# Late products of layer two's gated mixer: stores on POOL's queue, earlier requests for mixing blocks and bias rows, and the last row turned between two products

## The chip, the cores and the metric

The kernel runs on one core of a Trainium2 chip. The engines of a core work side by side: TensorE multiplies matrices (PE in the profile, and PEld for its weight loads), VectorE (DVE), ScalarE (ACT) and GpSimd (POOL) work on tiles, and SyncE (SP) only issues transfers between the chip's memory and the core's on-chip memory. Each engine takes its instructions in the order in which the program wrote them for it, and waits on semaphores for the others. The metric is device time of one execution in microseconds, lower is better; what is given is the median of several runs.

## The reference

Four blocks run one after the other on an input x of 2048 rows by 512 features: a linear attention block, a gated mixer, and the same two again with the same weights. Only the second mixer ("layer two", L = 1 in the kernel) is touched by the change. The mixer, in the reference's own words:

```python
def _B_ref(x, w_in, w_sp, b_sp, w_out):
    Fh = F // 2                                             # 896
    z = _gelu(jnp.einsum("bsd,df->bsf", x, w_in))
    z1 = z[..., :Fh]
    z2 = _layernorm(z[..., Fh:], axis=-1)
    g = jnp.einsum("ts,bsf->btf", w_sp, z2) + b_sp[None, :, None]
    return jnp.einsum("bsf,fd->bsd", z1 * g, w_out)
...
x = x + _A_ref(_layernorm(x, axis=-1), A_wqkv, A_wo)
x = x + _B_ref(_layernorm(x, axis=-1), B_w_in, B_w_sp, B_b_sp, B_w_out)
```

Everything is float32. So z1 (the gate) and z2 (what is mixed) are two halves of one product of x with `w_in`; z2 is normalised row by row; then the 2048 by 2048 matrix `w_sp` mixes all rows of z2, a bias per row is added, the result is multiplied by z1 and goes through `w_out`.

## The kernel before

**Numbers in two parts.** TensorE takes each float32 operand as a high part h (rounded, written by ACT in `high`, L213) and a low part l = x - h (written by DVE in `low`, L216). A product is three matmuls: h with h, h with l, l with h (L227 to L229 in `mm3`, L1142 to L1144 in `fmul`, L983 to L985 in `emul`, L1833 to L1835 in `acc`). Many products are also formed by Strassen's scheme with seven products of half size in place of eight (numbered r = 1 to 7 in the code), which need sums and differences of blocks first.

**Memory.** On-chip memory is given out by hand in slots that are used in turn, oldest free one first: 22 pages of 128 by 512 (`pages`, pg), 6 quads of four pages (`quads`, qd), 4 big ones (`bigs`, bg), the 16 tiles `ztile`, one for each 128 rows (z_z, z_y and z_q in the profile), and the 8 accumulator banks (`banks`). A new user of a slot waits for every reader and writer of the old one, transfers included.

**Order.** The program is one list written out by hand; there is no planner. Each engine and each queue executes its part of the list in that order, so an instruction that waits holds up everything behind it on its own engine. Plain transfers are issued by SP (`nc.sync.dma_start`). POOL issues those that convert the type or add (`nc.gpsimd.dma_start`), among them the loads of `w_in` parts in `load_r` (L202 to L205), which `wfetch` calls for two pages at a time.

**The stage around the change.** `P2.run2` goes through row blocks s = 1 to 18 of layer two. Odd steps are `odd`, even ones from 8 on are `epair`, which forms z2 of two row blocks and takes a list of callbacks to run between its products. Rows are turned (transposed) for the products: most through a store and a load in another shape, some, among them the last row block 15, on TensorE (`transposes`, L383), with a copy by DVE (L433), the high part by ACT and the low part by DVE (`d_high`, `d_low`). At the last odd step, s = 17, `odd` starts the products u[1] and u[2] of the third row group in `first_a` (each a product of six matmuls and a copy by ACT, L1159), adds the two halves of the third row group in `raw(0)` (DVE, L1149), turns row block 15 (through `q`, at its old place after `first_a(1, 2)`), and then finishes u[1] and u[2] in `first_b`. The last `epair`, s = 18, calls `late4`, which applies the gelu to them and stores them (`first_out`, `out`), and `late3`.

Then `P4.run` drives `P2.tail`, the late products: the last third of z1 for the last two row groups. `tail` is a generator with three stops. Its products are the six matmuls of `fmul` per f in 0, 1, 2 with five left operands one after the other (T5, T6, T7, x and T4), after a first product in `f`. After the first stop it applies gelu to c[0..2] and stores them, after the second to y[0..2], after the third to d[0..2], nine stores, all through `out` (L1130 to L1136) and before the change all issued by SP in L1134. The y and d results go into four spare pages, `room` (`Rooms`, handed out in turn): three y and the first d fill it, and the second and third d reuse places. Between the second and the third stop the last two tiles of z2, 14 and 15, are normalised by `e4` (L371, ACT).

At each stop `P4.run` prepares the mixing: `zahead` (`zsum` on DVE, L1728 to L1734, then `zpart`, ACT and DVE) prepares an operand from z2; `sp` (`wsp`, L1663 ACT and L1664 DVE) splits a mixing block into high and low part, in a quad of its own; `fetch` (L1643) asks SP for the next mixing blocks, 512 KB each. A raw block occupies half a quad (`Halves`), and its half is free again when `sp` has split it. The mixing products themselves are `mm`, step g = 0, 1, 2, ..., of twelve matmuls each (L1833 to L1835). In the loop over g, step g asks for block g + 5 and splits block g + 2 where that isn't done. The four bias rows are loaded by `loadb` (L1864, 256 KB each) at g = 0, and first needed when DVE adds them to the sums at the end of g = 3 (L1797).

Of the kernel before, what the change touches and what calls it, by code (L numbers as in the profile page):

```python
# [13 lines left out]
OP = mybir.AluOpType  # L14
# [5 lines left out]
NT = S // P  # L20
# [131 lines left out]
def mixer_kernel(ctx: ExitStack, tc: tile.TileContext, x_in, wqkv, wo_d, win1_d, win2_d, wsp_d, bsp_d, wout_d,  # L152
                 ident_d, mask_d, out_d):
    nc = tc.nc
# [7 lines left out]
    pages = Slots(main, "pg", 22)  # L162
    quads = Slots(main, "qd", 6)
    bigs = Slots(main, "bg", 4)
    banks = Banks(psum, "bank", 8)

    PAGE = [P, 512]
    ztile = {}
# [22 lines left out]
    z1s = {}  # L191
# [20 lines left out]
    def high(h, src):  # L212
        nc.scalar.activation(h, src, AF.Copy)  # L213
# [610 lines left out]
    class P2:  # L824
# [302 lines left out]
            nc.sync.dma_start(z1s[self.L, n, f], t)  # L1127
            home.put(t)

        def out(self, n, f, b, home=pages):  # L1130
            t = home.get(PAGE) if hasattr(home, "get") else home
            self.mark = nc.scalar.activation(t, b, AF.Gelu_apprx_tanh)
            z1s[self.L, n, f] = dram.tile(PAGE, F32, name=f"z1_{self.L}_{n}_{f}")
            nc.sync.dma_start(z1s[self.L, n, f], t)  # L1134
            if t is not home:
                home.put(t)  # L1136

# [29 lines left out]

        def first_out(self, *fs):
            for f in fs:
                self.out(2, f, self.u[f])  # L1170
                banks.done(self.u[f])
                if f:
                    self.wfetch()

        def T1(self):
            h, l = (t.bitcast(F32)[:, 0:2] for t in self.xT[3])
            t = self.B[:, 0]
            nc.vector.tensor_sub(t, h, t)
            nc.vector.tensor_add(t, t, l)
# [17 lines left out]
        def tail(self):  # L1197
            V, A = nc.vector, nc.scalar.activation
            h, l = (t.bitcast(F32) for t in self.xT[3])
            big = [bigs.get([P, NF, 512], F32R if k < 2 else F32) for k in range(3)]  # L1200
            c = [big[2][:, f] for f in range(3)]
            room = Rooms(big[2][:, f] for f in range(3, NF))
            two = lambda k, n: big[k][:, 2 * n:2 * n + 2]
            self.T |= {6: (two(0, 0), two(0, 1)), 7: (two(0, 2), two(1, 0)), 4: (two(1, 1), two(1, 2))}
            b21 = self.B[:, 1]
            for r, t in ((6, self.t2), (7, self.b22)):
                for k in range(2):
                    high(self.T[r][0][:, k], t[k])
                for k in range(2):
                    low(self.T[r][1][:, k], t[k], self.T[r][0][:, k])  # L1210
            for k in range(2):
                V.tensor_sub(b21[:, k], b21[:, k], self.t2[k])
            pages.put(*self.t2, *self.b22)
            self.f(True)
            ws, d = [], []
            for f in range(3):
                ws.append(self.ws.popleft())
                v = banks.get(PAGE)
                self.fmul(v, [t[:, 0:256] for t in ws[f]], self.T[5], True, True)
                A(c[f], v, AF.Copy)  # L1220
                banks.done(v)
            quads.put(self.T1q)
            self.fout()
            for f in range(3):
                y = self.y[f]
                self.fmul(y, [t[:, 256:512] for t in ws[f]], self.T[6], False, False)
                pages.put(*ws[f])
                self.wfetch()
                d.append(banks.whole(PAGE))
                A(d[f], y, AF.Copy)  # L1230
                V.tensor_add(y, y, c[f])
            split(*self.T[4], b21)
            self.e3(NT - 2)
            self.e3(NT - 1)
            self.e4(NT - 4)
            self.e4(NT - 3)
            quads.put(self.B)
            ws = []
            for f in range(3):
                ws.append(self.ws.popleft())  # L1240
                self.fmul(d[f], [t[:, 0:256] for t in ws[f]], self.T[7], False, False)
                V.tensor_add(c[f], d[f], c[f])
            yield
            for f in range(3):
                self.out(3, f + 3, c[f], c[f])
            x = [t[:, 2:4] for t in self.xT[3]]
            for f in range(3):
                self.fmul(self.y[f], [t[:, 256:512] for t in ws[f]], x, False, True)
                pages.put(*ws[f])
            yield  # L1250
            for f in range(3):
                self.out(3, f, self.y[f], room)
                banks.done(self.y[f])
            quads.put(*self.xT.pop(3))
            self.e4(NT - 2)
            self.e4(NT - 1)
            for f in range(3):
                w = self.ws.popleft()
                self.fmul(d[f], w, self.T[4], False, True)
                pages.put(*w)  # L1260
            yield
            for f in range(3):
                self.out(2, f + 3, d[f], room)
                banks.done(d[f])
            bigs.put(*big)

# [73 lines left out]
        def odd(self, s, p, q, r):  # L1340

            p()
            if s == NT - 1:
                self.first_a(0)
            if s == NT + 1:
                self.first_a(1, 2)
                self.B = quads.get([P, 2, 2, 512])
                self.raw(0)
            elif s - 5 >= FIRSTPAIR:
                self.e3(s - 5)  # L1350
                self.e3(s - 4)
            n = FILL.get(s, 0)
            if n:
                self.f(s == NT - 1, ZHome(s + 1) if s + 1 < NT else pages)
            if s == NT - 1:
                self.d_high(s - 2)
                self.d_low(s - 2)
            else:
                r()
            q()  # L1360
            if s - 4 < FIRSTPAIR:
                self.e4(s - 4)
            self.dsum(s - 3)
            self.dsplit(s - 3)
            if n > 2:
                self.f(home=ZHome(s + 2) if s + 2 < NT else pages)
            if n > 1:
                self.f(True)
            if s == NT - 1:
                self.first_b(0)  # L1370
                self.first_out(0)
            if s == NT + 1:
                self.first_b(1, 2)
                self.T1()
# [222 lines left out]
    class P4:  # L1597
# [559 lines left out]
        def run(self, nxt):  # L2157
            p2 = self.p2
            early = nxt is None
# [7 lines left out]
            n = 0  # L2167
            if early:
                for _ in p2.tail():
                    n += 1  # L2170
                    self.zahead(n - 1)
                    self.sp(n - 1)
                    if n < 3:
                        self.fetch(n + 1)
                self.zahead(3)
                self.fetch(5)
            while p2.f():
                self.zahead(min(self.zmade, 3))
                n += 1
# [11 lines left out]
            n = len(self.steps)  # L2191
            for g in range(n):
                p, k = self.steps[g]
                self.fetch(g + 5)
                evac_first = p == "P6" and k == HT - 1
                div_first = p in self.div and k == 13 and p == "P4"
                if not evac_first and not div_first:
                    self.sp(g + 2)
                    self.zahead(g + 4 if p in ("P2", "P1") else g + 4)
                self.mm(g)  # L2200
                if evac_first:
                    self.evac(p)
                    self.sp(g + 2)
                if not early and g == 14:
                    self.sums.fetch()
                if not early and 15 <= g <= 15 + LEFT:
                    self.sums.tick()
                if nxt is not None:
                    self.sums.halve(PARTS.get((p, k), -1), self.mark)
                if g == 0:  # L2210
                    self.loadb()
                if p in self.div:
                    if k % 2 == 1:
                        self.evac_div(p, self.SEVEN[k // 2])
                    if div_first:
                        self.sp(g + 2)
                    if k == 13 and p == "P4":
                        self.gq.extend((n, f) for n in range(2) for f in range(3))
                    continue
                if p == "P1" and k == 6:  # L2220
                    self.ask(3)
                self.tick()
                if p == "P3":
                    if k == FIRST:
                        self.first()
                self.wseven(p, k)
                if p == "P7" and k == HT - 1 and self.div:
                    self.sp(g + 3)
                if k == HT - 1 and not evac_first:
                    self.evac(p, (0,) if p == "P3" else (0, 1))  # L2230
# [82 lines left out]
```

## Time and profile before

| what | value |
|---|---|
| median of 3 runs | 1356.5 us (1356.29 to 1357.22) |
| the profiled execution's own time | 1356.72 us |
| its span in the profile | 1354.8 us |
| granted TensorE clock, mean | 0.999 |
| PE busy | 1345.7 us, 99% of the span |
| DVE busy | 1040.5 us, 77% |
| ACT busy | 717.2 us, 53% |
| POOL busy | 442.9 us, 33% |

The profile's times count from the start of the span. In a timeline a row gives start, duration, engine, line of the kernel, operation, the tiles written and read by name, and how many instructions of a kind are put together; in brackets stands how long the engine had sat idle before, and what ended that. Matmuls overlap, so a matmul is listed with 0.39 us although the next one starts much sooner: the distance between starts is what counts. SPq rows are the issue of a transfer, not the transfer.

### The profile page before, as it was taken

How to read it: one execution, taken by the hardware profiler on the slowest of the kernel's cores; microseconds unless marked ns; L12 is line 12 of the kernel's file. 1: busy time of each engine (PE TensorE's matmuls, PEld its weight loads, DVE VectorE, ACT ScalarE, POOL GpSimd, SP SyncE). 2: the span in 40 equal slices, each digit the busy share in tenths (PEclk: the TensorE clock that was granted, in tenths of full speed). 3: DMA queues.
4: the chain of work that ended last, by engine and by line, in shares of the span. 5: the costliest groups of instructions: out<-in, count | busy, mean ns of one | idle time of the engine just before them, and what ended most of it. 6: DMA issues, size and time to landing. Idle time of an engine off the chain costs nothing.

```text
span 1354.8 us, 19111 instructions
## 1 busy us (share of the span) xinstructions
PE 1345.7 (99%) x6564; PEld 1147.4 (85%) x6564; DVE 1040.5 (77%) x1640; ACT 717.2 (53%) x1199; POOL 442.9 (33%) x581
## 2 busy tenths in 40 slices
PE   9999999999999999999999999999999999999998
PEld 7888888888888888889988888888887888888898
DVE  6679877763796788898867878677678757988885
ACT  5774534433642364445667756565686333734454
POOL 3765775444031400201335334545430021021021
PEclk9999999999999999999999999999999999999999
DMA  5898587877877966533766513778647543455344
GB/s 182 280 320 274 162 273 249 294 271 255 288 248 256 279 201 182 192 132 63 173 179 202 181 53 119 234 226 272 209 149 267 166 170 126 155 186 173 107 73 68
DMA packets 161777, 267.21 MB, mean 197 GB/s; under 512 B 13712, under 2 KB 53136, under 8 KB 161552
## 3 DMA queue, kind: packets, MB, share of 16 engines
q1 hardware_dynamic: 148144, 240.04, 53.2%
q0 software_dynamic: 13536, 25.96, 9.3%
q8 instruction: 51, 0.84, 0.2%
q14 instruction: 46, 0.38, 0.1%
HBM read 187.30 MB, written 87.03 MB: 202 GB/s over the span
## 4 chain that ended last, share of the span: by engine, by line
PE 95%; DVE 1%; ACT 1%; DMA 1%; issue 1%; SPq 0%; DVEq 0%; ACTq 0%
PE bank L229 14%; PE bank L227 14%; PE bank L228 14%; PE bank L1834 13%; PE bank L1835 13%; PE bank L1833 13%; PE bank L2031 3%; PE bank L2032 3%; PE bank L2033 3%; PE bank L983 1%; PE bank L985 1%; PE bank L984 1%; PE bank L383 1%; PE bank L2045 1%; PE bank L2044 1%
## 5 line engine op out<-in xcount | busy, mean ns | idle before, releaser
L1834 PE MATMUL bank<-qd,pg 128*128 128x512 f32 x768 | 299.7, 390 | 1.2 <-DVE qd L1664 1.2
L1833 PE MATMUL bank<-qd,pg 128*128 128x512 f32 x768 | 299.4, 390 | 1.4 <-ACT qd L1663 1.4
L1835 PE MATMUL bank<-qd,pg 128*128 128x512 f32 x768 | 299.3, 390 | 0.0
L1663 ACT ACTIVATE qd<-qd 128x1024 fp32r<-128x1024 f32 x136 | 143.1, 1053 | 132.6 <-PE bank L1835 117.9
L1664 DVE TENSOR_TENSOR qd<-qd,qd 128x1024 fp32r<-128x1024 f32 x136 | 171.5, 1264 | 54.1 <-ACT qd L1663 53.7
L229 PE MATMUL bank<-qd,pg 128*128 128x512 f32 x448 | 174.7, 390 | 0.0
L1833 PEld LDWEIGHTS bank<-qd,pg 128*128 128x128 f32 x768 | 144.6, 188 | 32.0 <-ACT qd L1663 1.8
L1834 PEld LDWEIGHTS bank<-qd,pg 128*128 128x128 f32 x768 | 144.6, 188 | 31.3 <-DVE qd L1664 1.5
L1835 PEld LDWEIGHTS bank<-qd,pg 128*128 128x128 f32 x768 | 144.6, 188 | 29.8
L1874 POOL TENSOR_TENSOR bg<-bg,pg 128x512 f32<-128x512 f32 x28 | 50.3, 1798 | 304.2 <-ACT qd L1663 174.1
L227 PE MATMUL bank<-qd,pg 128*128 128x512 f32 x308 | 120.2, 390 | 0.2 <-ACT pg L213 0.2
L228 PE MATMUL bank<-qd,pg 128*128 128x512 f32 x308 | 120.0, 390 | 0.0
L229 PEld LDWEIGHTS bank<-qd,pg 128*128 128x128 f32 x448 | 84.1, 188 | 18.2 <-DVE pg L216 0.4
L362 POOL TENSOR_SCALAR rs<-mv 128x1 f32<-128x1 f32 x80 | 24.6, 308 | 192.3 <-DVE mv L360 179.3
L371 ACT ACTIVATE pg<-pg,nb,rs 128x512 f32<-128x512 f32 x52 | 42.1, 811 | 85.1 <-POOL nb L365 79.4
L1573 POOL TENSOR_TENSOR pg<-pg,pg 128x512 f32<-128x512 f32 x48 | 67.1, 1398 | 59.8 <-DMA pg<-in_wsp_dram 57.7
L2033 PE MATMUL bank<-wo,qd 128*128 128x256 f32 x288 | 81.5, 283 | 0.0
L2031 PE MATMUL bank<-wo,qd 128*128 128x256 f32 x276 | 78.1, 283 | 0.0
L2032 PE MATMUL bank<-wo,qd 128*128 128x256 f32 x276 | 78.0, 283 | 0.0
L213 ACT ACTIVATE pg<-pg 128x512 fp32r<-128x512 f32 x77 | 47.9, 624 | 50.0 <-DVE pg L447 18.0
L1703 ACT ACTIVATE pg<-pg 128x384 fp32r<-128x384 f32 (+1 forms) x32 | 18.5, 579 | 100.0 <-DVE pg L1701 54.7
L228 PEld LDWEIGHTS bank<-qd,pg 128*128 128x128 f32 x308 | 57.8, 188 | 12.2 <-DVE qd L216 0.3
(262 smaller groups left out, 3248.9 us busy)
## 6 DMA issues: line engine op xcount, KB each, us to landing
qd<-s SPq DMA_DIRECT2D x64, 512.0 KB, 3.7
qd<-in_wsp_dram SPq DMA_DIRECT2D x40, 512.0 KB, 3.8
qd<-hP SPq DMA_DIRECT2D x32, 512.0 KB, 3.9
pg<-z SPq DMA_DIRECT2D x56, 256.0 KB, 3.9
pg<-in_wsp_dram SPq DMA_DIRECT2D x52, 256.0 KB, 4.4
s<-pg SPq DMA_DIRECT2D x48, 256.0 KB, 3.8
z<-pg SPq DMA_DIRECT2D x39, 256.0 KB, 3.2
pg<-w POOLq DMA_DIRECT2D x38, 256.0 KB, 4.7
```

The lines of the kernel that those rows point to most:

```text
L227: nc.tensor.matmul(out, ah, bh, start=start, stop=False)
L228: nc.tensor.matmul(out, ah, bl, start=False, stop=False)
L229: nc.tensor.matmul(out, al, bh, start=False, stop=stop)
L1573: nc.gpsimd.tensor_tensor(t, a, b, op=OP.add)
L1663: self.mark = nc.scalar.activation(w[:, 0], r, AF.Copy)
L1664: nc.vector.tensor_sub(w[:, 1], r, w[:, 0].bitcast(F32))
L1833: m(out, h[:, o], w[:, 0, j, :], start=start, stop=False, skip_group_check=True)
L1834: m(out, h[:, o], w[:, 1, j, :], start=False, stop=False, skip_group_check=True)
L1835: m(out, l[:, o], w[:, 0, j, :], start=False, stop=stop, skip_group_check=True)
L2031: m(out, A, x, start=start and f == 0, stop=False, skip_group_check=True)
L2032: m(out, A, y, start=False, stop=False, skip_group_check=True)
L2033: m(out, B, x, start=False, stop=stop and f == 2, skip_group_check=True)
```

## The change

1. `out` issues its store on POOL's queue unless it is told otherwise. With SP stay u[0] (in `first_out(0)`) and the last three, d[0..2]. On POOL go u[1], u[2], c[0..2] and y[0..2], eight stores.
2. `first_out` asks for the weight pages of u[1] and u[2] before it issues the two stores, not between them.
3. d[0..2] go into ordinary pages, no longer into `room`.
4. `loadb` is called near the head of `tail` (layer two only) and no longer at g = 0.
5. Mixing blocks 2 and 3 are asked for in `tail`, ahead of T7, in a second quad; after the first stop block 4 is asked for (it was 2), after the second block 5 (it was 3). The request for blocks 4 and 5 at the end goes.
6. The two quads of the fourth row group are given back before the second stop, not after it.
7. The normalisation of tiles 14 and 15 moves from ACT to DVE (`tensor_scalar`).
8. At s = 17 row block 15 is turned after `first_a(1)` and `raw(0)`, ahead of `first_a(2)`.

```diff
-        def out(self, n, f, b, home=pages):
+        def out(self, n, f, b, home=pages, by=None):
             t = home.get(PAGE) if hasattr(home, "get") else home
             self.mark = nc.scalar.activation(t, b, AF.Gelu_apprx_tanh)
             z1s[self.L, n, f] = dram.tile(PAGE, F32, name=f"z1_{self.L}_{n}_{f}")
-            nc.sync.dma_start(z1s[self.L, n, f], t)
+            (by or nc.gpsimd).dma_start(z1s[self.L, n, f], t)
...
         def first_out(self, *fs):
             for f in fs:
-                self.out(2, f, self.u[f])
-                banks.done(self.u[f])
                 if f:
                     self.wfetch()
+            for f in fs:
+                self.out(2, f, self.u[f], by=None if f else nc.sync)
+                banks.done(self.u[f])
...
             pages.put(*self.t2, *self.b22)
+            self.p4.loadb()
             self.f(True)
...
             quads.put(self.B)
+            self.p4.fetch(3)
             ws = []
...
                 pages.put(*ws[f])
+            quads.put(*self.xT.pop(3))
             yield
             for f in range(3):
                 self.out(3, f, self.y[f], room)
                 banks.done(self.y[f])
-            quads.put(*self.xT.pop(3))
-            self.e4(NT - 2)
-            self.e4(NT - 1)
+            for i in (NT - 2, NT - 1):
+                _, rs, nb = self.zms.pop(i)
+                V.tensor_scalar(ztile[i], ztile[i], rs, nb, op0=OP.mult, op1=OP.add)
...
             for f in range(3):
-                self.out(2, f + 3, d[f], room)
+                self.out(2, f + 3, d[f], by=nc.sync)
                 banks.done(d[f])
...
             if s == NT + 1:
-                self.first_a(1, 2)
+                self.first_a(1)
                 self.B = quads.get([P, 2, 2, 512])
                 self.raw(0)
+                q()
+                self.first_a(2)
...
-            q()
+            if s <= NT:
+                q()
...
                     if n < 3:
-                        self.fetch(n + 1)
+                        self.fetch(n + 3)
                 self.zahead(3)
-                self.fetch(5)
...
-                if g == 0:
+                if not early and g == 0:
                     self.loadb()
```

## The prediction

> **What bounds the kernel now.** I read first what TensorE waited for over the whole execution (each row: microseconds in total, times, longest), then the timeline of PE around the longest waits, then the windows for its clock (PEclk is the third number from the end).
>
> ```profile
> PE bank L616 <- DVE pg L611: 2.3, 1, 2.3
> PE bank L1833 <- ACT qd L1663: 1.4, 1, 1.4
> PE bank L1834 <- DVE qd L1664: 1.2, 1, 1.2
> ```
>
> ```profile
> 1009.05 0.39 PE L1142 MATMUL bank<-bg,pg 128*128 128x512 f32 x1
> 1013.13 0.39 PE L1833 MATMUL bank<-qd,pg 128*128 128x512 f32 x1
> 1021.06 0.39 PE L1835 MATMUL bank<-qd,pg 128*128 128x512 f32 x1
> 1022.85 0.50 PE L1833 MATMUL bank<-qd,pg 128*128 128x512 f32 x1 [1.40 <-ACT qd L1663]
> 1024.52 0.80 PE L1834 MATMUL bank<-qd,pg 128*128 128x512 f32 x1 [1.17 <-DVE qd L1664]
> ...
> 1028.00 0.39 PE L1833 MATMUL bank<-qd,pg 128*128 128x512 f32 x1
> ```
>
> ```profile
> 1024.50:1027.90 3.40, 3.38 (x8) 2.73 (x9) 1.93 (x3) 2.12 (x4) 0.00 (x0) 0.50 0.93 308
> ```
>
> But for the start (L616), TensorE stands in one place only, where a mixing product waits for ACT's and then DVE's half of its block. Its pace is 18 matmuls from 1009.05 to 1013.13, 0.227 us each. From 1021.06 to 1028.00 lie ten steps, due in 2.27 us and done in 6.94: **4.67 us are lost**, 1.56 before L1833, 1.44 before L1834 and 1.67 in eight steps at half clock. Mixing starts at 1013.13 with twelve matmuls (2.72 us) a step, so the late one is g = 3, due at 1021.29. ACT, DVE and SP show why.
>
> ```profile
> 1012.81 2.16 ACT L371 ACTIVATE z_z<-z_z,acc 128x896 f32<-128x896 f32 x2
> 1014.86 0.63 ACT L213 ACTIVATE pg<-pg 128x512 fp32r<-128x512 f32 x1
> 1019.59 1.23 ACT L1132 ACTIVATE bg<-bank 128x512 f32<-128x512 f32 x2 [2.67 <-DMA z<-bg]
> 1021.75 1.04 ACT L1663 ACTIVATE qd<-qd 128x1024 fp32r<-128x1024 f32 x1
> 1012.66 0.76 DVE L1728 TENSOR_TENSOR pg<-z_z 128x256 f32<-128x256 f32 x2
> 1015.52 0.69 DVE L216 TENSOR_TENSOR pg<-pg,pg 128x512 fp32r<-128x512 f32 x1 [2.11 <-ACT pg L213]
> 1016.47 1.23 DVE L1664 TENSOR_TENSOR qd<-qd,qd 128x1024 fp32r<-128x1024 f32 x1 [0.26 <-ACT qd L1663]
> 1021.37 0.69 DVE L216 TENSOR_TENSOR pg<-pg,pg 128x512 fp32r<-128x512 f32 x1 [3.00 <-ACT pg L213]
> 1023.25 1.22 DVE L1664 TENSOR_TENSOR qd<-qd,qd 128x1024 fp32r<-128x1024 f32 x1
> 1009.64 0.37 SPq L1643 DMA_DIRECT2D qd<-hP  x1
> 1013.19 7.97 SPq L1134 DMA_DIRECT2D z<-bg  x6
> 1021.25 0.95 SPq L1643 DMA_DIRECT2D qd<-hP  x2
> ```
>
> ACT normalises from 1012.81 to 1014.86 (2.05 us) and later stands 2.67 us, because the second d needs a place of `room` whose store hasn't landed. So its split for g = 3 comes at 1021.75, and DVE's, idle behind ACT three times, at 1023.25. SP sits in six stores until 1021.2 and asks for blocks 4 and 5 only then.
>
> **The change part by part.**
>
> *d into ordinary pages, normalisation on DVE (3, 7).* ACT loses the 2.05 and the 2.67. Counted through the program's gets and puts of slots, the three free pages that d will take were last read by the x products, which end at 1009.05, so nothing is awaited. ACT's split for g = 3 is then no longer what is late, and DVE paces. What its new work costs is bounded by two groups (mean ns after the busy time):
>
> ```profile
> L758 DVE TENSOR_SCALAR pg<-pg 128x512 f32<-128x512 f32 x2 | 0.8, 417 | 0.0
> L371 ACT ACTIVATE z_z<-z_z,acc 128x896 f32<-128x896 f32 x16 | 17.4, 1126 | 0.0
> ```
>
> The same operation at 417 ns scaled by 896/512 is 0.73 us, two are 1.46; ACT's own time for that shape gives 2.25. All that DVE has ahead of the end of the split for g = 3 runs from 1012.66 to 1024.47 (1023.25 + 1.22), with 2.11 + 0.26 + 3.00 = 5.37 idle. Without that it ends at 1019.10, with the new work at 1020.6 to 1021.4. TensorE needs the high half at 1021.29 and this low half one matmul on, at 1021.52: 0.1 to 0.9 us of cover. I take 1.46, the row of the same engine and operation, and so **-4.67**: both waits go, and with them, no idle time being left, the half clock.
>
> *Blocks 2 to 5 asked for earlier, quads back sooner (5, 6).* What would be late next is block 4, due on TensorE at 1021.29 + 2.72 = 1024.0 and asked for at 1021.25 before. It now takes the half quad that the split for g = 0 gives back, as block 2 does at 1009.64 today, and block 5 the next; even 7 us later both are there. Block 6 waits for the split of g = 2, some 1017, and is due at 1029.5. The early return of the two quads is to readers that end at 1009.05, ahead of the split for g = 2 that takes one. No cost; without this part the first stall would only uncover a second.
>
> *The request for 2 and 3 itself.* It goes out on SP behind the store of `fout`, near 998.5 to 999.5: 1 MB beside the last pair of weight pages that POOL loads. The rows are the POOL issue, its time to landing here and the longest one in the same kind of load (last number), the product that reads it, and the window (DMA share and GB/s last).
>
> ```profile
> 998.61 1.15 POOL L204 DMA_DIRECT2D pg<-w1s  x2
> pg<-w1s POOLq DMA_DIRECT2D x2, 256.0 KB, 3.3
> pg<-w1s POOLq DMA_DIRECT2D x1, 256.0 KB, 6.8
> 1003.61 0.39 PE L1142 MATMUL bank<-bg,pg 128*128 128x512 f32 x1
> 997.00:1004.00 7.00, 7.00 (x32) 5.80 (x31) 4.75 (x8) 5.11 (x10) 6.12 (x12) 1.00 0.72 199
> ```
>
> The second page is issued near 999.19, lands at 1002.5 and is read by the third matmul of its product, 1003.61 + 0.45 = 1004.06: 1.6 us to spare. With 6.8 it would land at 1006.0, 1.9 late. The window moves 199 x 7.0 = 1.39 MB; with 1.05 more it is 2.44 MB, 349 GB/s, above the 308 of the busiest row above, but these two pages stand first in POOL's queue. Between 0 and 1.9 I take **+0.2**, near the row of this very load. Six half-sized pages behind them are read from 1009.05 on and have twice that room.
>
> *Stores on POOL (1, 2).* Eight issues leave SP. POOL's next work behind the two u stores was idle until ACT released it:
>
> ```profile
> 991.43 0.73 POOL L1083 TENSOR_SCALAR acc<-acc 128x1 f32<-128x1 f32 x1 [11.13 <-ACT pg L1081]
> ```
>
> Two issues at some 0.58 (half of 1.15) fit into those 11 us, the weight pages now being asked for ahead of them. Behind the six c and y stores the list gives POOL nothing before the gates of the mixed sums (it is at 0.00 in the window with half clock). What could lose its cover is on the other side: c and y lie in big tiles that the mixed sums reuse at the end of g = 3, near 1024. Issued by 1015, they land by 1022 at 6.8. No cost.
>
> *Bias rows sooner (4).* SP issues them after blocks 0 and 1, near 991 to 993. Two of the four pages held u[1] and u[2], so SP, which is in order, waits for POOL's stores of these to land; behind it stand the store of `fout` and block 2, which ACT first reads past 1013. The four pages stay taken through `tail`; the free list doesn't run out (four free at the tightest, at the first stop), and the pages that move up the list were all last used early enough but one, which lets ACT wait 0.3 us or less for DVE in a place where it waits for TensorE anyway. No cost, and on SP the four requests no longer stand ahead of block 6.
>
> *Row 15 turned between two products (8).* ACT, DVE and PE at s = 17, and the two other waits of weight loads in this stage:
>
> ```profile
> 977.18 1.07 ACT L1159 ACTIVATE bank<-bank 128x512 f32<-128x512 f32 x2
> 978.70 0.63 ACT L213 ACTIVATE qd<-z_y 128x512 fp32r<-128x512 f32 x1 [0.45 <-DVE z_y L433]
> 976.85 1.22 DVE L1149 TENSOR_TENSOR qd<-qd,qd 128x1024 f32<-128x1024 f32 x1
> 977.98 0.68 DVE L433 COPY z_y<-bank 128x512 f32<-128x512 f32 x1
> 977.30 0.60 PE L383 MATMUL bank<-ident,z_y 128*128 128x128 f32 x4
> 977.83 0.50 PE L1142 MATMUL bank<-qd,pg 128*128 128x512 f32 x1
> ```
>
> ```profile
> PEld bank L983 <- DVE z_z L1027: 0.5, 1, 0.5
> PEld bank L985 <- DVE bg L216: 0.4, 1, 0.4
> ```
>
> The transposes come 1.36 us sooner (six matmuls). But the copy L433 starts at 977.98 because DVE is in `raw(0)` until then, and `raw(0)` stays ahead of it: row 15 is no earlier. ACT's order changes, though: the high half (978.70, waiting for L433) now stands ahead of the second copy L1159, which then runs from 979.23 to 979.8 and not before 978.3. `first_b(2)` adds into the bank that this copy reads. TensorE gets there at 977.30 - 1.36 + 0.53 + 2 x 1.36 = 979.2, and stands 0.6 us: a new wait of L1142 on ACT L1159. Part comes back: L985 waits 0.4 and L983 0.5 soon after for a DVE chain that is no later than before. Between 0 and 0.6, or -0.9 if both waits vanish, I take **+0.2**.
>
> *Sum:* -4.67 + 0.2 + 0.2 = -4.3. The profiled execution took 1356.72 (its span and 1.9 around it), 0.2 above the median: 1352.4 for such a one, **1352.2** for the median.
>
> **The rivals.** About 0.2% (2.7 us) is what can be told from no change; that is 1353.8 and 1359.2.
>
> *DVE becomes the bound.* The two normalisations take 2.25 and meet POOL's y stores, which are issued from 1012 to 1014; if they exclude each other, each of the two waits for one issue (0.58). 1019.10 + 3.4 = 1022.5, 1.0 late: 1353.2. For it: the cover is thin. Against: nothing in this trace shows a DVE operation lengthened beside a POOL issue. The Trainium skill has such a rule, on its page "SBUF — State Buffer", section "Who interferes with whom": a DVE operation in a two-port mode and a GpSimd instruction lock each other out for the whole instruction, and `tensor_scalar` can take that mode; no run here shows the pair together.
>
> *The weights come late.* 1.9 us as above: gain 2.6, 1353.9. If the idle time also halves the clock for 3.4 us, as two waits of 3.0 together did, 0.9, 1355.6. For it: 72% of the DMA time is taken already. Against: 1.6 us to spare.
>
> *The change doesn't do what it says.* Another block or operand is as late as g = 3 was, and the stall moves on by a step or two: 1356. For it: ACT, DVE and SP all were late at 1021. Against: each has 0.1 us or more by the sums above.
>
> *Slower.* POOL's stores of c and y land late, the gate sums that reuse their tiles wait on DVE at the end of g = 3, and every split behind them on DVE, too. It decides from landings past 1024 and TensorE's 2.7 us of split blocks; to end 2.7 us above today it must cost 7 us, landings near 1034, 19 us after the issue, and then the half clock on top: 1360. Against: 6.8 is the longest such time quoted here.
>
> **How the numbers follow.** The forecast has 0.68 (own range 1351.0 to 1353.2: below it both costs nil, 0.4, half of the 0.9 gained, and 0.4 between executions; above it the weights late by 0.8 in place of 0.2, and the same 0.4), DVE 0.09, late weights 0.10, no effect 0.05, slower 0.08. Faster is the first two, 0.77; the next two are within 0.2%, 0.15. From 1351.0 up to 1354.4 lie the first two and most of the third, 8 in 10.
>
> **What would show it.** Right: no PE wait on L1663 or L1664, the clock full from 1013 to 1060, no ACT wait on a store at L1132, L1643 twice near 999, a wait of some 0.6 at L1142 on ACT L1159 near 979. Wrong: a wait of L1142 at L204's pages near 1004, idle time before L1834 at g = 3, DVE idle on a store before L1797.

## The result and the profile after

The changed kernel takes **1354.12 us** (median of 14 runs, 1352.91 to 1355.37); the kernel before took 1356.52 in the runs beside it (14 runs, 1354.64 to 1358.52). The ratio is 0.9981 with a 95% interval of 0.9973 to 0.9989: 2.4 us faster (1.5 to 3.7), where 4.3 were forecast. The profiled execution took 1353.14 (span 1351.4), 3.58 less than the profiled one of before.

The view that was read first, what TensorE waited for, of the kernel after (microseconds in total, times, longest). It holds two rows now: the start of the program, and a wait that was not there before. The waits on the splits (L1663 and L1664 before) are gone.

```profile
PE bank L616 <- DVE pg L611: 2.3, 1, 2.3
PE bank L1144 <- DMA pg<-w1s: 0.5, 1, 0.5
```

Two windows of the kernel after, the first over the time in which the kernel before had half its clock, the second over the whole start of mixing (PEclk is the third number from the end):

```profile
1024.50:1027.90 3.40, 3.40 (x17) 2.82 (x16) 3.40 (x8) 1.58 (x2) 0.00 (x0) 1.00 0.77 253
1013.00:1060.00 47.00, 47.00 (x209) 38.94 (x208) 45.60 (x73) 28.71 (x43) 0.80 (x2) 1.00 0.72 230
```

PE is busy without a gap and at full clock. The timeline of PE, ACT, DVE and POOL around the third mixing step shows why (start, duration, engine, line, operation, tiles; in brackets idle time before and what ended it; the splits of blocks are L1670 and L1671 now, the mixing products L1840 to L1842):

```profile
1013.57 0.39 PE L1840 MATMUL bank<-qd,pg 128*128 128x512 f32 x1
...
1021.73 0.39 PE L1840 MATMUL bank<-qd,pg 128*128 128x512 f32 x1
1021.96 0.39 PE L1841 MATMUL bank<-qd,pg 128*128 128x512 f32 x1
```

```profile
1013.91 1.57 ACT L1132 ACTIVATE pg<-bank 128x512 f32<-128x512 f32 x3
1017.33 1.05 ACT L1670 ACTIVATE qd<-qd 128x1024 fp32r<-128x1024 f32 x1
1012.28 1.40 DVE L1260 TENSOR_SCALAR z_z<-z_z,acc 128x896 f32<-128x896 f32 x2
1018.55 1.22 DVE L1671 TENSOR_TENSOR qd<-qd,qd 128x1024 fp32r<-128x1024 f32 x1
1011.88 1.92 POOL L1134 DMA_DIRECT2D z<-bg  x3 [1.38 <-ACT bg L1132]
```

Step g = 3 starts at 1021.73, exactly 36 matmuls after 1013.57 (36 x 0.2267 = 8.16). ACT writes the three d without waiting for a place, and its split for g = 3 begins at 1017.33 (1021.75 before). DVE's split ends at 1018.55 + 1.22 = 1019.77 and is needed at 1021.96: 2.2 us of cover.

What was lost in its place is earlier, in the first product of T7. Timeline of PE, then the landing of the second page that POOL loads there (KB, and microseconds from issue to landing), both of the kernel after:

```profile
1003.46 0.39 PE L1143 MATMUL bank<-bg,pg 128*128 128x512 f32 x1
1004.33 0.50 PE L1144 MATMUL bank<-bg,pg 128*128 128x512 f32 x1 [0.48 <-DMA pg<-w1s]
1004.67 0.40 PE L1142 MATMUL bank<-bg,pg 128*128 128x512 f32 x1
```

```profile
pg<-w1s POOLq DMA_DIRECT2D x1, 256.0 KB, 5.4
```

The product's third matmul stands until the page lands, 5.4 us after its issue where it took 3.3 before. From 1003.46 to 1004.67 lie two steps, due in 0.45 and done in 1.21.

To see all that changed in one line per execution I count the 6564 matmul starts in order and measure four stretches between the same matmuls. "Up to there" is from the first matmul to row block 15's stage (the 4601st); "turn" from the 4669th to the 4791st, s = 17 and 18; "weights" from there to the 4835th, the products T7 to T4 but for the ends; "mixing" from there to the 4931st, which holds g = 0 to 7 (its first two steps still belong to T4). What lies between and behind these is the same in all (14.4 and 311.6). All microseconds.

| profiled execution | its time | up to there | turn | weights | mixing |
|---|---|---|---|---|---|
| before | 1356.72 | 958.75 | 27.21 | 9.97 | 26.43 |
| after | 1353.14 | 959.31 | 26.29 | 10.79 | 21.76 |

So after minus before is +0.56 - 0.92 + 0.82 - 4.67 = -4.21; with +0.78 behind the last matmul this is the -3.4 by which the span is shorter. The +0.56 and the +0.78 lie in code that the change doesn't touch.

### The profile page after: what moved, and what is told of

The parts are those of the page before. It is cut to its first block, busy times and chain, and to the rows that moved or that the text cites. A ratio compares the mean times of both kernels' runs of the same rounds, so it can differ in the third digit from the quotient of the medians.

```text
span 1351.4 us, 19108 instructions
## 1 busy us (share of the span) xinstructions
PE 1343.9 (99%) x6564; PEld 1146.4 (85%) x6564; DVE 1039.8 (77%) x1642; ACT 715.1 (53%) x1197; POOL 448.0 (33%) x589
## 4 chain that ended last, share of the span: by engine, by line
PE 98%; DVE 1%; DMA 0%; issue 0%; POOL 0%; ACT 0%; DVEq 0%; POOLq 0%; ACTq 0%
PE bank L229 14%; PE bank L228 14%; PE bank L227 14%; PE bank L1842 13%; PE bank L1840 13%; PE bank L1841 13%; PE bank L2038 3%; PE bank L2039 3%; PE bank L2040 3%; PE bank L984 1%; PE bank L985 1%; PE bank L983 1%; PE bank L383 1%; PE bank L2052 1%; PE bank L2051 1%; PE bank L2053 1%
## 5 line engine op out<-in xcount | busy, mean ns | idle before, releaser
L1840 PE MATMUL bank<-qd,pg 128*128 128x512 f32 x768 | 298.8, 389 | 0.0
L1842 PE MATMUL bank<-qd,pg 128*128 128x512 f32 x768 | 298.8, 389 | 0.0
L1671 DVE TENSOR_TENSOR qd<-qd,qd 128x1024 fp32r<-128x1024 f32 x136 | 171.2, 1262 | 54.9 <-ACT qd L1670 54.9
L1670 ACT ACTIVATE qd<-qd 128x1024 fp32r<-128x1024 f32 x136 | 143.2, 1053 | 131.8 <-PE bank L1842 120.4
L1842 PEld LDWEIGHTS bank<-qd,pg 128*128 128x128 f32 x768 | 144.2, 188 | 29.9
L1840 PEld LDWEIGHTS bank<-qd,pg 128*128 128x128 f32 x768 | 144.2, 188 | 29.8
L227 PE MATMUL bank<-qd,pg 128*128 128x512 f32 x308 | 120.2, 390 | 0.0
```

The source lines that it names most:

```text
L227: nc.tensor.matmul(out, ah, bh, start=start, stop=False)
L1670: self.mark = nc.scalar.activation(w[:, 0], r, AF.Copy)
L1671: nc.vector.tensor_sub(w[:, 1], r, w[:, 0].bitcast(F32))
L1840: m(out, h[:, o], w[:, 0, j, :], start=start, stop=False, skip_group_check=True)
L1842: m(out, l[:, o], w[:, 0, j, :], start=False, stop=stop, skip_group_check=True)
```

## The experiments

A ratio is to the kernel before, run in the same session, with its 95% interval; stretches are those of the table above.

**Both kernels once more.** No edit; one more profile of each.

> The kernel before once more, for a second profile. The profiled pair differs by 4.26 us on TensorE's last matmul, the medians by 2.4 us. Theory A, the stall of before varies: the two waits at g = 3 (1.56 and 1.44 us in the first profile) come again within 0.5 us, but the half clock (1.67 us) need not, so the loss between the starts of the third and the fifth mixing step is 3.0 to 4.7 us here. Rival B, the stall of before is always the same 4.7 us and it is the changed kernel that varies: 4.5 to 4.8 us here, half clock included.

> The changed kernel once more, for a second profile. Theory A: no wait at g = 3, a wait for the weight pages near 1004 of 0.4 to 1.2 us (0.75 in the first profile), and no wait at s = 17 and 18 beyond 0.3 us. Rival B: the wait for the weight pages or the one at s = 17 is 2 us or more here.

The kernel before took 1354.68 us. Its waits of PE from 940 to 1060 and four rows of its timelines of ACT and PE:

```profile
PE bank L1834 <- DVE qd L1664: 1.9, 3, 1.2
```

```profile
1017.78 1.24 ACT L1132 ACTIVATE bg<-bank 128x512 f32<-128x512 f32 x2 [1.01 <-DMA z<-bg]
1022.73 0.50 PE L1834 MATMUL bank<-qd,pg 128*128 128x512 f32 x1 [1.17 <-DVE qd L1664]
1029.89 1.06 ACT L1663 ACTIVATE qd<-qd 128x1024 fp32r<-128x1024 f32 x1 [2.69 <-DMA qd<-in_wsp_dram]
1032.27 0.50 PE L1834 MATMUL bank<-qd,pg 128*128 128x512 f32 x1 [0.59 <-DVE qd L1664]
```

The store that ACT waits for landed sooner (1.01 us of idle time, not 2.67), only the low half was late at g = 3, and the clock stayed full. Between the starts of the third and the fifth step 1.49 us are lost, less than either theory had. Its mixing stretch is 24.63, 2.87 above 21.76 and not 4.67: the rest is lost at g = 4 (0.50) and g = 6 (0.88), behind an ACT that waits for the block itself to land (the row of 1029.89 is the split for g = 6). The prediction's reading of one place, g = 3, doesn't hold for this execution. The kernel after took 1355.69; its weights stretch is 11.38, longer than the first time, and its mixing stretch 21.76 again: theory A, although the 1.41 us lost at the weights are a little more than it had.

**The kernel before a third time.**

> The kernel before once more, to see how far its stall at the late steps of mixing varies. Theory (the stall is set by when SP's stores into room land, and halves the clock only where two waits of more than 1 us follow each other): the part from the first mixing product takes 24.5 to 26.5 us against 21.76 without a stall, and the half clock shows only with the longer stalls. Rival (the 4.67 us of the first profile are the rule): 26.4 again, with half clock.

1355.04 us, mixing stretch 25.07, turn 27.13, weights 9.97. Timeline of PE, and ACT's split of block 4:

```profile
1022.74 0.50 PE L1834 MATMUL bank<-qd,pg 128*128 128x512 f32 x1 [1.17 <-DVE qd L1664]
1025.90 0.50 PE L1833 MATMUL bank<-qd,pg 128*128 128x512 f32 x1 [0.38 <-ACT qd L1663]
1027.16 0.50 PE L1834 MATMUL bank<-qd,pg 128*128 128x512 f32 x1 [0.76 <-DVE qd L1664]
1024.79 1.06 ACT L1663 ACTIVATE qd<-qd 128x1024 fp32r<-128x1024 f32 x1 [2.21 <-DMA qd<-hP]
```

Here the stall is split over two steps, 2.10 us at g = 3 and 1.15 at g = 4, the second because block 4 comes late; no half clock. Over three executions the stalls of mixing are worth 4.67, 2.87 and 3.31 us: the first profile was the dearest, and in the two others between a third and a half of the loss lies behind late blocks. That half the clock goes only with the long stall of the first fits these three executions and no more.

**d back into `room`.**

```diff
-                self.out(2, f + 3, d[f], by=nc.sync)
+                self.out(2, f + 3, d[f], room, by=nc.sync)
```

> The changed kernel with the three d results back in the spare pages (room), all else as changed. Theory, the place in room is what held ACT: ACT waits 2 to 3.5 us for a store at L1132 again, its split for g = 3 comes 2 to 3.5 us later than in the changed kernel, and TensorE loses 0.5 to 2 us at g = 3 to 5; 0.05 to 0.15% over the changed kernel. Rival, with the normalisation gone from ACT the wait is covered: ACT waits, TensorE doesn't.

1354.11 us, ratio 0.9981 (0.9972 to 0.9991), like the whole change. In its timeline ACT waits for places again, and its waits of weight loads show a late split:

```profile
1018.33 0.60 ACT L1132 ACTIVATE bg<-bank 128x512 f32<-128x512 f32 x1 [2.43 <-DMA z<-bg]
```

```profile
PEld bank L1841 <- DVE qd L1671: 0.6, 1, 0.6
```

The mixing stretch is 22.18: 0.42 us lost, all of it at g = 3. With the normalisation off ACT, the wait for a place nearly fits into the cover in this execution, closer to the rival than to the theory.

**The normalisation back on ACT.**

```diff
-            for i in (NT - 2, NT - 1):
-                _, rs, nb = self.zms.pop(i)
-                V.tensor_scalar(ztile[i], ztile[i], rs, nb, op0=OP.mult, op1=OP.add)
+            self.e4(NT - 2)
+            self.e4(NT - 1)
```

> The changed kernel with tiles 14 and 15 normalised on ACT again. Theory, thin cover: ACT's split for g = 3 comes 2.0 us later, DVE's 1.0 to 1.5 us later, and TensorE loses 0 to 0.5 us at g = 3. Rival, the normalisation was half of the stall: TensorE loses 1 us or more.

1354.01 us, ratio 0.9984 (0.9974 to 0.9993). Timeline of ACT and POOL (lines from L1260 on are one less here):

```profile
1013.06 2.16 ACT L371 ACTIVATE z_z<-z_z,acc 128x896 f32<-128x896 f32 x2
1019.20 1.04 ACT L1669 ACTIVATE qd<-qd 128x1024 fp32r<-128x1024 f32 x1
1012.50 1.61 POOL L1134 DMA_DIRECT2D z<-bg  x3 [1.38 <-ACT bg L1132]
```

ACT's split for g = 3 begins at 1019.20 in place of 1017.33 and is in time; the mixing stretch is 21.76. Either of the two edits to ACT's work alone removes all or nearly all of the stall: they were worth 4.67 us together in the first profile, and not a part each. Each rests on one profile of a wait that varies.

**Blocks 2 to 5 asked for at their old places.**

```diff
             quads.put(self.B)
-            self.p4.fetch(3)
...
-                        self.fetch(n + 3)
+                        self.fetch(n + 1)
                 self.zahead(3)
+                self.fetch(5)
```

> The changed kernel with mixing blocks 2 to 5 asked for where they were before: block 2 after the first stop, 3 after the second, 4 and 5 behind the last. Theory of the prediction: the wait for weight pages near 1004 goes (0.7 to 1.4 us in the profiles so far), and a wait of 0.3 to 1.5 us comes at g = 4 or 5 for blocks 4 and 5. Rival, SP is free so early now that blocks 4 and 5 are in time: no wait at either place, and this is faster than the changed kernel by 0.7 us or more.

1356.03 us, beside 1356.29 for the kernel before; ratio 0.9991 (0.9981 to 1.0): half of the gain or more is gone. Waits of PE from 940 to 1060, the timeline of ACT, and the landing of the second weight page:

```profile
PE bank L1840 <- DVE qd L1670: 0.8, 1, 0.8
PE bank L1839 <- ACT qd L1669: 0.5, 1, 0.5
```

```profile
1025.05 1.06 ACT L1669 ACTIVATE qd<-qd 128x1024 fp32r<-128x1024 f32 x1 [2.65 <-DMA qd<-hP]
```

```profile
pg<-w1s POOLq DMA_DIRECT2D x1, 256.0 KB, 3.4
```

ACT now waits 2.65 us for block 4 itself, the mixing stretch is 23.63 (1.87 lost, 1.21 of it at g = 4), and the wait at T7 is gone: its page lands in 3.4 us, the weights stretch is 9.97. So the early request pays for itself and is what slows the page: the bias rows and POOL's stores are at their new places in this kernel, too.

**Blocks 2 and 3 asked for together with 0 and 1**, at the end of s = 18 and not in `tail`.

```diff
             quads.put(self.B)
-            self.p4.fetch(3)
...
                 if s == NT + 2:
-                    self.p4.fetch(1)
+                    self.p4.fetch(3)
```

> The changed kernel, with mixing blocks 2 and 3 asked for together with 0 and 1 at the end of s = 18, ahead of the bias rows, and no longer beside the last pair of weight pages. Theory: the new wait near 1004 (0.75 us) comes from the 1 MB of blocks 2 and 3 beside those pages; it falls to 0 to 0.2 us, and the time by 0.5 to 0.8 us against the changed kernel: ratio to before 0.9975 to 0.9979. Rival, the pages are late whatever runs beside them since POOL issues them behind its own small operations: the wait stays at 0.5 us or more and the ratio at 0.998.

1352.95 us, ratio 0.9975 (0.9966 to 0.9985). No wait of PE at T7, weights stretch 9.98, mixing 21.76. The landing of the second weight page:

```profile
pg<-w1s POOLq DMA_DIRECT2D x1, 256.0 KB, 4.6
```

It lands later than the 3.3 us of before, beside the four blocks and the bias rows (3 MB) asked for 5 to 9 us ahead of it, but 4.6 us is in time.

**The weight pages asked for sooner.** One more `wfetch` in `late4`, ahead of the two u stores; all else as after.

```diff
                                 self.wfetch()
+                                self.wfetch()
                                 self.first_out(1, 2)
```

> The kernel after, with one pair of weight pages more asked for on POOL's queue in late4, ahead of the two u stores; mixing blocks 2 and 3 are still asked for behind the store of fout, near 998.5. Theory A (the third matmul of T7's first product, L1144, waits because POOL asks for its page near 999 and the page lands beside 1 MB on SP's queue): asked for some 10 us sooner, the page is there; the wait of 0.5 to 0.9 us at L1144 on w1s and what else is lost near 1003 to 1006 (0.75 to 1.4 us) go, the third part (T7 to T4) takes 9.97 us as in the kernel before, ratio 0.997 to 0.9978, as with the blocks asked for first. Theory B (SP's megabyte slows any load of weights in this stretch, whatever the time of the request): the wait moves to the next pages, read from 1009, and the part takes 10.7 to 11.4 us as in the kernel after.

**1351.15 us**, ratio 0.9962 (0.995 to 0.9975), the lowest median of all (5 runs). In its timeline of POOL the pair goes out with the four pages before it, nearly twenty microseconds sooner; SP asks for the blocks at the old place (this whole execution runs some 2 us behind the first one of the kernel after):

```profile
979.27 3.22 POOL L204 DMA_DIRECT2D pg<-w1s  x6
```

```profile
1000.14 14.63 SPq L1651 DMA_DIRECT2D qd<-hP  x4
```

PE waits for nothing from 940 to 1060, the weights stretch is 9.97: theory A. The wait doesn't move to the next pages. The median lies 3.0 us below the changed kernel's, though, and the weights stretch accounts for 0.8 to 1.5 of them; where the rest comes from isn't shown.

**Both requests sooner**, the two edits above together.

> Both requests sooner: blocks 0 to 3 together at the end of s = 18, and the pair of weight pages in late4. If either alone removes the whole wait of L1144 on w1s, both together give no more than either: third part 9.97 us, ratio 0.997 to 0.9978. If some of it is left with one alone, 0.2 to 0.4 us less than that.

1352.25 us, ratio 0.997 (0.9958 to 0.9982), weights stretch 9.97. No more than either alone, as their stretches say; the intervals of the three overlap, so the order of their medians isn't settled.

**Bias rows at g = 0 again.**

```diff
             pages.put(*self.t2, *self.b22)
-            self.p4.loadb()
...
-                if not early and g == 0:
+                if g == 0:
                     self.loadb()
```

> The kernel after, but the bias rows are asked for at g = 0 again. Theory (the early request only takes four pages and some SP time, no one waits for it): no difference that can be told, within 0.1% of the kernel after, no PE wait from 1013 to 1060. Rival (SP, in order, stands at the bias rows till POOL's stores of u land, which puts the request for blocks 2 and 3 beside the weight pages): with the rows back at g = 0, blocks 2 and 3 are asked for several us sooner, near 991, and the wait of L1144 on w1s goes, 0.75 to 1.4 us less.

1354.57 us, ratio 0.9987 (0.9978 to 0.9996): no difference from the change. Its timeline of SP, and its wait at T7:

```profile
998.02 0.34 SPq L1127 DMA_DIRECT2D z<-pg  x1
998.40 14.62 SPq L1649 DMA_DIRECT2D qd<-hP  x4
```

```profile
PE bank L1144 <- DMA pg<-w1s: 1.2, 1, 1.2
```

The blocks are asked for at the same time without the bias rows ahead of them: what holds SP until 998 is the store of `fout`, and the rival falls.

**Stores issued by SP again.**

```diff
-            (by or nc.gpsimd).dma_start(z1s[self.L, n, f], t)
+            (by or nc.sync).dma_start(z1s[self.L, n, f], t)
```

> The changed kernel with all nine stores and those of u issued by SP again, all else as changed. Theory of the prediction: the queue of the stores costs and brings nothing, since nothing that SP has behind them is needed soon: no wait at g = 3 to 6, the same time as the changed kernel within 0.05%. Rival, SP standing on the gelus asks for blocks 4 to 7 too late: TensorE waits at g = 4 to 7, 0.5 us or more.

1353.96 us, ratio 0.9981 (0.9972 to 0.9991): the same as the change, mixing stretch 21.76. Timeline of SP:

```profile
1013.01 2.19 SPq L1134 DMA_DIRECT2D z<-bg  x3
1015.29 2.53 SPq L1134 DMA_DIRECT2D z<-pg  x3
1017.92 2.21 SPq L1650 DMA_DIRECT2D qd<-in_wsp_dram  x2
```

The six stores of y and d take 4.8 us now, not 7.97, since none waits for an ACT that itself waits for a place, and no block that is due soon stands behind them. Both together, the stores on SP and d in `room`, wasn't tried.

**Row 15 turned at its old place.** The edit undoes part 8 of the change.

```diff
-                self.first_a(1)
+                self.first_a(1, 2)
                 self.B = quads.get([P, 2, 2, 512])
                 self.raw(0)
-                q()
-                self.first_a(2)
...
-            if s <= NT:
-                q()
+            q()
```

> The changed kernel with the turn of row block 15 back at its old place, behind both first_a. The prediction had the new place cost 0.2 us (0 to 0.6); the first profile of the changed kernel shows a gain of 0.9 us up to the end of s = 18. Theory, the move gains when the load of row block 14 lands early, since DVE then isn't in raw(0) when the transposes are done: here the waits at s = 17 and 18 come back, 0.6 to 1.0 us in all, and the ratio to before is 0.9985 to 0.999. Rival, the gain is the chance of an early load alone and has nothing to do with the place: the waits stay under 0.3 us where the load is early, ratio 0.998.

1355.16 us, ratio 0.9991 (0.9983 to 1.0); the interval overlaps that of the change, and it is the stretch that tells. The turn stretch is 27.12, as before, 0.83 longer than after. Timelines of DVE, of this kernel and of the kernel after:

```profile
975.33 1.22 DVE L1149 TENSOR_TENSOR qd<-qd,qd 128x1024 f32<-128x1024 f32 x1
977.86 0.69 DVE L433 COPY z_y<-bank 128x512 f32<-128x512 f32 x1 [1.32 <-PE bank L383]
```

```profile
975.96 1.22 DVE L1149 TENSOR_TENSOR qd<-qd,qd 128x1024 f32<-128x1024 f32 x1
977.14 0.69 DVE L433 COPY z_y<-bank 128x512 f32<-128x512 f32 x1
```

At the old place the copy waits 1.32 us for TensorE's transposes, behind a `raw(0)` that was done 1.3 us before. At the new place it follows `raw(0)` without a wait. The kernel before shows the 1.32 in its second and third profile, too (turn 27.12 and 27.13); only in its first one a load of row 14 held DVE (the row with L447), so that `raw(0)` was late and covered it:

```profile
974.44 1.10 DVE L447 STREAM_TRANSPOSE z_y<-pg 128x512 f32<-128x512 f32 x1 [1.48 <-DMA pg<-yt]
```

Where that load is late with the new place, the wait that was forecast appears. The waits of PE in the kernel with the normalisation back on ACT, in which DVE stood 1.14 us at L447:

```profile
PE bank L1142 <- ACT bank L1159: 0.2, 1, 0.2
```

Its turn stretch is 26.81, those of the kernels with blocks late or asked for together, where DVE stood 0.92 and 0.96 us at L447, 26.58 and 26.69: still 0.3 to 0.6 less than before. In these two the wait shows only in the weight loads of L1142 (0.4 and 0.5 us).

All profiled executions together, by the same stretches:

| kernel | its time | up to there | turn | weights | mixing |
|---|---|---|---|---|---|
| before, second | 1354.68 | 958.70 | 27.12 | 9.97 | 24.63 |
| before, third | 1355.04 | 958.62 | 27.13 | 9.97 | 25.07 |
| after, second | 1355.69 | 960.79 | 26.33 | 11.38 | 21.76 |
| d in `room` | 1354.46 | 960.70 | 26.29 | 11.06 | 22.18 |
| normalisation on ACT | 1353.38 | 959.40 | 26.81 | 11.17 | 21.76 |
| blocks late | 1356.25 | 960.88 | 26.58 | 9.97 | 23.63 |
| blocks with first | 1353.01 | 959.17 | 26.69 | 9.98 | 21.76 |
| weights sooner | 1353.58 | 961.33 | 26.29 | 9.97 | 21.76 |
| both sooner | 1351.23 | 958.92 | 26.33 | 9.97 | 21.76 |
| bias rows back | 1354.41 | 959.59 | 26.28 | 11.47 | 21.76 |
| stores on SP | 1352.89 | 959.25 | 26.29 | 11.01 | 21.76 |
| turn back | 1353.99 | 958.68 | 27.12 | 11.35 | 21.76 |

## Why the prediction was right, and where not

The sign and the mechanism of the gain were right, and the time lies in the range (1351.0 to 1354.4), near its upper end: above the forecast's own 1351.0 to 1353.2, and by the number alone nearest to the rival of late weights (1353.9). Three of the terms were mis-sized, one of them with the wrong sign; the errors at the weights and at the turn offset each other, which is luck.

- **The stall of -4.67.** All of it went, as argued: no wait on the splits, no half clock. But "the half clock" and the 1.40 before L1833 belonged to one execution; only the 1.17 before L1834 came in all three. Two more of the same kernel lost 2.87 and 3.31 in mixing, in part at g = 4 and g = 6, where the blocks themselves were late. By the mean of the three the gain is some 3.6, not 4.67. This step failed in size, by taking one profile's stall as the kernel's. ("In one place only" also passes over a wait of 0.2 us at L227, early in the same profile.)
- **DVE's cover of 0.1 to 0.9 us.** The two normalisations took 1.40, 1.46 was taken. The cover came out at 2.2: DVE was through with the split ahead 0.37 sooner than before (1011.14 for 1011.51, the start), TensorE came 0.44 later (1013.57 for 1013.13), and DVE's list, the two normalisations included, ran 0.4 us shorter than summed (7.49 for 7.90). The 0.37 and the 0.44 together are what TensorE lost at T7: in the kernel with the weights asked for sooner, which loses nothing there, the cover is 1.4. DVE didn't become the bound.
- **Blocks earlier, "without this part the first stall would only uncover a second".** Shown: with the blocks at their old places 1.87 us are lost, most of them one step on, and half of the gain or more goes. The kernel before loses at these later steps, too, in two of its three executions.
- **The request for 2 and 3, +0.2 between 0 and 1.9.** This is the step that failed in the other direction: "near the row of this very load", I took a load that had the queue almost to itself as the measure for one beside a megabyte. The second page needed 5.4 us (3.3 before, 1.6 to spare), and the weights stretch is 0.82 to 1.50 us longer in the seven executions that have SP's request beside POOL's. Asking for the blocks earlier, later, or for the pages earlier each removes it, which settles the cause. That the pages "stand first in POOL's queue" was no protection. The rival of late weights had the mechanism, at 0.82 to 1.50 of its 1.9; the clock didn't fall.
- **Stores on POOL: no cost.** Confirmed, and no gain either: with them on SP, and d in pages of its own, the time is the same.
- **Bias rows: no cost.** Confirmed; the blocks wait for `fout`'s store either way.
- **Row 15, +0.2.** Wrong in sign. "The copy L433 starts at 977.98 because DVE is in `raw(0)` until then" held only for the profile at hand, where row 14's load was late. Otherwise the copy was bound by the transposes, and they do come earlier: -0.8, and -0.3 to -0.6 with that load late by 0.9 us or more, in spite of the new wait of L1142.
- **The two-port rival.** Its bound, one issue of 0.58 per normalisation, wasn't needed: the two L1260 took 1.40 beside three POOL issues, 0.74 us each, and 0.74 each as well in the kernel with the stores on SP, where POOL issues none. The Trainium skill, on its page "SBUF — State Buffer", section "Who interferes with whom", lets the one that is issued later wait. For the second and third y store that would be POOL, as each begins while a normalisation runs: the three take 1.92 (0.54, 0.73 and 0.67) with the normalisations on DVE and 1.61 (0.54 each) with them on ACT. The direction agrees; the size (0.31, beside 1.40 of DVE work) is less than a block for a whole instruction would be, and the first store, issued 0.40 ahead of the first normalisation and still running at its start, didn't lengthen that. Nobody waits for these stores.

By stretches the terms are then -3.6 for mixing, +1.2 for the weights (the mean of the seven, 11.18, less 9.97) and -0.8 for the turn, together -3.2 where -4.3 was summed. The measured 2.4 has an interval of 1.5 to 3.7 us, which holds it. What is left, 0.8, is open, and two stretches in code that the change doesn't touch differ by as much. What lies behind the last matmul takes 4.16 us in the three executions of the kernel before and 4.16 to 5.37 in the eleven others (4.71 in the mean). And the stretch "up to there" is 958.6 to 958.8 in the four executions that turn row 15 at the old place and 958.9 to 961.3 in the ten others. All these differences of "up to there" arise before 330 us, at waits in code that is the same in all kernels. Whether either is chance or goes with the kernel wasn't tried. It also is why the profiled execution of the kernel with the lowest median (1353.58, "up to there" 961.33) says less on its worth than that median.

## What to carry to other kernels

A stall that depends on when a transfer lands is a distribution: before summing with one profile's value, read it from two or three executions, and ask of each "bound by" whether the releaser itself was late that time. A bulk request that is moved earlier must be checked against every small load that lands in the same few microseconds on other queues, with a landing time under load and not the one seen alone. Where the small load can be asked for earlier at no cost, do that: here that removed the whole 1.2 us, in the kernel with the lowest median measured.

## What the runs showed of the hardware

- A load on one queue lands later beside another queue's transfers: the same 256 KB on POOL's queue landed in 3.3 us with one store of 256 KB on SP's, in 4.6 with 3 MB of SP's asked for 5 to 9 us ahead, and in 5.4 with 1 MB asked for within 0.4 us of it.
- Two waits of TensorE of 1.40 and 1.17 us in a row were followed by 3.4 us at half clock; three waits of 1.17, 0.38 and 0.76 us within 6 us were not.
- Three store issues on POOL took 1.92 us beside two DVE `tensor_scalar` operations on 128 by 896 elements, and 1.61 without them; the DVE operations took 0.74 us each with and without the stores, where scaling a narrower one by its width gave 0.73.
